# Twelve wide products of zeros in place of forty-eight narrow ones at the start of TensorE's stream

## The chip, the cores and the metric

The kernel runs on one core of a Trainium2 chip. The metric is the device time of one execution in microseconds (us), the median of several runs. Each core has TensorE (PE; its weight loads are listed apart as PEld), VectorE (DVE), ScalarE (ACT), GpSimd (POOL) and SyncE (SP, which issues nearly all the DMAs here). They run in parallel, each through its own list of instructions in order, and wait for one another by semaphores.

## The reference, cut to what matters

Two stages follow one another. The first is a linear attention with a decaying state, for 4 batches, 8 heads, 768 positions and a head of 48:

```python
for t in range(S):
    cur = np.einsum('bhd,bhe->bhde', u[None] * kt, vt)
    y[:, :, t] = np.einsum('bhd,bhde->bhe', rt, state + cur)
    state = wt[:, :, :, None] * state + np.einsum('bhd,bhe->bhde', kt, vt)
```

The second takes y as 3072 tokens of 384 numbers through two matrices (384 to 2048, 2048 to 384) with a piecewise quadratic gate between them:

```python
h = x @ w_in
g = np.where(h >= 1, h, np.where(h <= -1, 0.0, (h + 1) ** 2 / 4))
return g @ w_out
```

The products of zeros that this document is about are not part of either stage. They write zeros to PSUM banks before those are used.

## The kernel before, in words

Attention is done in 12 units of 256 positions (three for each batch), each in chunks of 64. For a unit, DVE scans the decays forward and backward (lines 439 and 434, tiles p and y) and scales r and k with the results (lines 518 and 468, tile rk). TensorE multiplies r and k within a chunk (line 488), transposes k (line 527), forms the states' updates (line 549) and then the outputs (line 598). The second stage takes 512 tokens at a time (256 in parts of the first blocks), and for each of 16 slices of the weights makes nine products into h (line 960) and nine into acc (line 980). Each number is split in two parts of lower precision, and three products of such parts are added. The weights are loaded raw and decoded once, on ACT, POOL and DVE (lines 356 to 369).

The order of instructions on each engine is set before the program runs, by a planner (class Plan). It is given a cost in us and a due time for each operation, goes through them as a machine with five engines would, and writes them out in the order in which they began there.

The change is in the first operation of TensorE, the function warm (lines 322 to 328), which the planner treats as one piece. It runs as soon as GpSimd has filled the tiles zero and clear with zeros. It makes SMALL products of the fp32 tile zero, each with 64 rows of weights and 64 columns of weights. Number n takes the upper or lower half of the partitions of zero by n % 2, and the upper or lower half of the output's partitions by n // 2 % 2. So four consecutive products use the four quarters of the array. All go to the first two banks. Then one product of 128x128 by 512 columns goes to each of the 8 PSUM banks (the function cleared, line 331). Wherever the planner sees a gap on TensorE of over 0.5 us, it puts further products of line 331 in (functions kept_warm and zeros).

The planner's cost of warm is a constant, 0.16 + 0.054 * SMALL + 0.43 * 8. The profile has two of line 331's products ahead of the ones of line 325, and six more behind the eight of warm.

Of the kernel before, what the change touches and what calls it, by code (L numbers as in the profile page):

```python
# [24 lines left out]
C = 64  # L25
NC = UT // C
SEG = 2 * (UT + 1)
HP = 64
# [9 lines left out]

LAG = 2
IDLE, FILLED, ZEROS = 0.5, 0.72, 0.235  # L40
SMALL = 48

LANES = 8

# [195 lines left out]
def attention_moe(tc, a):  # L240
    nc = tc.nc
    V, A, G, PE = nc.vector, nc.scalar, nc.gpsimd, nc.tensor
# [7 lines left out]
    def tiles(n, shape, dt, name, of=pool):  # L250
        return [of.tile(shape, dt, tag=f"{name}{i}", name=f"{name}{i}") for i in range(n)]

    def one(shape, dt, name, of=pool):
        return tiles(1, shape, dt, name, of)[0]
# [10 lines left out]
    zero = one([128, 128], F32, "zero")  # L265
    clear = one([128, 128], F32R, "clear")
# [25 lines left out]
    bank = [*tiles(3, [128, 512], F32, "bank", psum), *acc, *hp]  # L292

    def op(engine, cost, due, reads, writes, emit, **kw):
        return plan.add(engine, cost, emit, due, reads, writes, **kw)
# [8 lines left out]
    SOON = 0, 200.0  # L304
# [17 lines left out]
    def warm():  # L322
        for n in range(SMALL):
            g, h = n // 2 % 2, n % 2
            PE.matmul(bank[h][HP * g : HP * g + C, 0:C], lhsT=zero[HP * h : HP * h + HP, 0:C], rhs=zero[HP * h : HP * h + HP, 0:C],
                      start=True, stop=True)
        for b in bank:
            cleared(b, 4)

    def cleared(out, n):  # L330
        PE.matmul(out[:, 0 : 128 * n], lhsT=clear, rhs=clear.unsqueeze(1).broadcast_to([128, n, 128]), start=True, stop=True)  # L331

    op("PE", 0.16 + 0.054 * SMALL + 0.43 * 8, SOON, ["zero", "clear"], [("b", i) for i in range(8)], warm)

    def zeros(b, us):
        halves = int(FILLED * us / ZEROS * 2)
# [713 lines left out]
```

## Time and profile before

| | us |
|---|---|
| median of 3 runs | 505.94 |
| lowest and highest run | 504.72, 509.08 |
| profiled execution, its own time | 508.8 |
| span of that execution, first to last instruction | 507.1 |
| TensorE busy in the span | 492.8 |
| VectorE busy | 332.2 |
| ScalarE busy | 296.1 |
| GpSimd busy | 100.4 |

The profile is of one execution. Its span begins with its first instruction, and every position given in this document counts from there. The time of an execution is 1.7 us longer than its span, for what lies around the first and the last instruction. An fp32 product stands in the profile as two matmul records and two weight loads, so that the 48 products of line 325 are 96 records.

### The profile page before, as it was taken

What the parts mean: (1) busy time and instruction counts of PE and PEld (TensorE: products, weight loads), DVE (VectorE), ACT (ScalarE), POOL (GpSimd) and SP (SyncE); (2) the same over time, 40 slices, a digit from 0 to 9 for tenths busy, and PEclk for the clock granted to TensorE, in tenths of its full rate; (3) what the DMA queues carried; (4) which work ended last, traced back from release to release, by engine and by line L of the source; (5) the groups of instructions that cost most, each with busy time, mean ns of one, the idle gap of its engine ahead of it and who ended that gap; (6) DMA issues with size and microseconds to landing.
All of it is one profiled execution on the core that took longest, in us unless ns stands there. A gap on an engine that the chain in (4) does not pass through costs nothing.

```text
span 507.1 us, 13246 instructions
## 1 busy us (share of the span) xinstructions
PE 492.8 (97%) x5562; PEld 412.5 (81%) x5562; DVE 332.2 (66%) x560; ACT 296.1 (58%) x605; POOL 100.4 (20%) x68
## 2 busy tenths in 40 slices
PE   8999999999999999999999899999999999999995
PEld 6778987889999988888878678888887888888884
DVE  6899997956998699849555979842364333243331
ACT  3597798987875564745643565653454444454441
POOL 2487766801012321102001112100010000000000
PEclk9999999999999999999999999999999999999999
DMA  8984734326643434505006342300110000100001
GB/s 297 403 296 147 281 145 153 126 64 208 201 126 97 140 108 143 167 11 204 23 1 193 106 134 90 123 1 1 63 49 13 17 1 0 63 2 0 1 1 67
DMA packets 21922, 54.12 MB, mean 107 GB/s; under 512 B 3104, under 2 KB 8672, under 8 KB 21856
## 3 DMA queue, kind: packets, MB, share of 16 engines
q1 hardware_dynamic: 21856, 53.21, 31.5%
q8 instruction: 45, 0.74, 0.6%
q14 instruction: 21, 0.17, 0.1%
HBM read 46.32 MB, written 4.72 MB: 101 GB/s over the span
## 4 chain that ended last, share of the span: by engine, by line
PE 75%; DVE 13%; DMA 4%; ACT 3%; issue 3%; SPq 1%; ACTq 0%; DVEq 0%
PE h L960 33%; PE acc L980 33%; PE bank L598 4%; DVE y L434 2%; DVE gl L768 2%; PE bank L488 2%; DMA rk<-in_rk 2%; DVE p L439 1%; DMA wraw<-in_wbits 1%; DVE wt L369 1%; PE bank L527 1%; PE bank L549 1%; DVE r L494 1%; DMA wq<-in_w 1%; DVE g L765 1%
## 5 line engine op out<-in xcount | busy, mean ns | idle before, releaser
L960 PE MATMUL h<-x,wt 128*128 128x512 f32 (+1 forms) x1008 | 216.8, 361 | 1.9 <-DVE g L765 1.3
L960 PEld LDWEIGHTS h<-x,wt 128*128 128x128 f32 x1008 | 168.3, 188 | 31.8 <-DVE g L765 1.9
L980 PE MATMUL acc<-gh,wt 128*128 128x512 f32 (+1 forms) x672 | 152.2, 360 | 0.0
L980 PEld LDWEIGHTS acc<-gh,wt 128*128 128x128 f32 x672 | 113.8, 188 | 19.0
L765 DVE SCALAR_TENSOR_TENSOR g<-g,h 128x512 f32<-128x512 f32 (+1 forms) x112 | 67.4, 605 | 92.1 <-ACT g L764 84.9
L763 ACT ACTIVATE g<-h 128x512 f32<-128x512 f32 (+1 forms) x112 | 59.7, 533 | 85.8 <-PE h L960 84.1
L768 DVE TENSOR_TENSOR gl<-g,gh 128x512 fp32r<-128x512 f32 (+1 forms) x112 | 73.3, 659 | 28.9 <-ACT gh L767 13.5
L767 ACT CAST gh<-g 128x512 fp32r<-128x512 f32 (+1 forms) x112 | 62.1, 558 | 39.6 <-PE acc L980 18.6
L980 PE MATMUL acc<-gl,wt 128*128 128x512 f32 (+1 forms) x336 | 84.5, 357 | 0.1
L980 PEld LDWEIGHTS acc<-gl,wt 128*128 128x128 f32 x336 | 58.4, 187 | 10.0 <-DVE gl L768 0.5
L764 ACT ACTIVATE g<-g 128x512 f32<-128x512 f32 (+1 forms) x112 | 64.0, 571 | 3.3
L364 POOL TENSOR_SCALAR rr<-wraw 128x768 uint16<-128x768 f32 x16 | 52.7, 3291 | 35.0 <-DVE fl L366 17.3
L514 POOL TENSOR_TENSOR r<-cst,d 128x512 f32<-128x512 f32 x16 | 17.3, 1104 | 157.0 <-PE bank L598 131.9
L506 POOL TENSOR_TENSOR nk<-nk 128x768 f32<-128x768 f32 x8 | 16.8, 2096 | 83.7 <-DMA nk<-in_nk 74.5
L439 DVE TENSOR_TENSOR_SCAN p<-wq,seeds 128x514 f32<-128x514 f32 x24 | 30.2, 1259 | 3.7 <-DMA wq<-in_w 2.8
L434 DVE TENSOR_TENSOR_SCAN y<-wq,seeds 128x514 f32<-128x514 f32 x24 | 30.8, 1282 | 0.8
L468 DVE TENSOR_TENSOR rk<-rk,y 128x512 f32<-128x512 f32 x24 | 18.9, 789 | 3.1 <-DMA rk<-in_rk 2.9
L331 PE MATMUL bank<-clear 128*128 128x512 f32 (+1 forms) x57 | 17.1, 418 | 1.8 <-DVE seeds L438 1.8
L369 DVE TENSOR_TENSOR wt<-fl,wt 128x768 fp32r<-128x768 f32 x16 | 16.5, 1033 | 3.2 <-ACT wt L356 3.1
L598 PEld LDWEIGHTS bank<-rk,st 48*48 48x48 f32 (+1 forms) x656 | 11.4, 121 | 8.6 <-DVE st L567 2.9
L363 ACT ACTIVATE rr<-wraw 128x768 uint16<-128x768 uint32 x16 | 17.5, 1094 | 1.1 <-DVE fl L366 1.1
L518 DVE TENSOR_TENSOR rk<-rk,p 128x512 f32<-128x512 f32 x24 | 17.7, 749 | 0.2 <-PE acc L488 0.2
(108 smaller groups left out, 384.5 us busy)
## 6 DMA issues: line engine op xcount, KB each, us to landing
rk<-in_rk SPq DMA_DIRECT2D x24, 512.0 KB, 4.8
wraw<-in_wbits SPq DMA_DIRECT2D x16, 768.0 KB, 7.9
wq<-in_w SPq DMA_DIRECT2D x24, 257.5 KB, 3.3
nk<-in_nk SPq DMA_DIRECT2D x8, 768.0 KB, 4.8
vn<-in_v SPq DMA_DIRECT2D x11, 384.0 KB, 5.8
fl<-in_w SPq DMA_DIRECT2D x12, 257.0 KB, 2.9
out_y<-g SPq DMA_DIRECT2D x11, 256.0 KB, 2.3
x<-last SPq DMA_DIRECT2D x66, 32.0 KB, 2.5
```

The source lines that it names most:

```text
L364: op("POOL", 3.35, due, [("raw", f)], ["rr_high"], lambda: G.tensor_scalar(out=r16[:, :, 1], in0=wraw[f][:, :, 1].bitcast(F32), scalar1=0. ...
L369: op("DVE", 0.95, due, [("fl", k), ("wh", f)], [("wl", f)], lambda: V.tensor_tensor(out=w_lo[f], in0=s, in1=w_hi[f].bitcast(F32), op=ALU.s ...
L434: V.tensor_tensor_scan(out=y_[:, ::-1], data0=w[:, SEG:0:-1], data1=sv[:, ::-1], initial=0.0, op0=ALU.mult, op1=ALU.add)
L439: V.tensor_tensor_scan(out=pv[:, q].rearrange("p n c -> p (n c)"), data0=w[:, 0:SEG], data1=sv, initial=0.0, op0=ALU.mult, op1=ALU.add,)
L598: PE.matmul(out=bank[by[g]][HP * half : HP * half + wide, lo : lo + C], start=first, stop=False, skip_group_check=True, **kw)
L763: op("ACT", c, due, [("b", 6 + hk)], [("g", gk)], lambda: nc.scalar.activation(gs, hs, AF.Relu, scale=0.5, bias=0.5))
L764: op("ACT", c, due, (), [("g", gk)], lambda: nc.scalar.activation(gs, gs, AF.Square))
L765: op("DVE", 0.13 + 0.56 * k, due, [("b", 6 + hk)], [("g", gk)], lambda: nc.vector.scalar_tensor_tensor(out=gs, in0=gs, scalar=1.0, in1=hs, ...
L767: op("ACT", c, due, [("g", gk)], [("gh", gk)], lambda: nc.scalar.copy(ghs, gs))
L768: op("DVE", 0.18 + 0.52 * k, due, [("g", gk), ("gh", gk)], [("gl", gk)], lambda: nc.vector.tensor_tensor(out=gls, in0=gs, in1=ghs.bitcast( ...
L960: nc.tensor.matmul(by16(hp, f), lhsT=wx[f][:, cs], rhs=by16(xt[:, j, :], f), start=n == 0, stop=n == 8)
L980: nc.tensor.matmul(by16(o[j]), lhsT=wx[f][:, cs], rhs=by16(gt), start=first and i == 0, stop=stop and i == 2, skip_group_check=True)
```

## The change

The number of the first products goes from 48 to 12, and each streams 256 columns in place of 64. The 256 columns are the same 64 columns of the tile zero, read four times over by a broadcast dimension. The weights, the halves of the partitions and the two banks that are written stay as they are; in these banks the columns 0 to 255 are written now, and not only 0 to 63. The planner's cost for each is four times what it was, so that the sum of warm comes out as before: 0.054 * 48 and 0.216 * 12 are both 2.592.

```diff
-SMALL = 48
+SMALL = 12
...
         for n in range(SMALL):
             g, h = n // 2 % 2, n % 2
-            PE.matmul(bank[h][HP * g : HP * g + C, 0:C], lhsT=zero[HP * h : HP * h + HP, 0:C], rhs=zero[HP * h : HP * h + HP, 0:C],
-                      start=True, stop=True)
+            PE.matmul(bank[h][HP * g : HP * g + C, 0 : 4 * C], lhsT=zero[HP * h : HP * h + HP, 0:C],
+                      rhs=zero[HP * h : HP * h + HP, 0:C].unsqueeze(1).broadcast_to([HP, 4, C]), start=True, stop=True)
...
-    op("PE", 0.16 + 0.054 * SMALL + 0.43 * 8, SOON, ["zero", "clear"], [("b", i) for i in range(8)], warm)
+    op("PE", 0.16 + 0.216 * SMALL + 0.43 * 8, SOON, ["zero", "clear"], [("b", i) for i in range(8)], warm)
```

TensorE's list becomes 36 products shorter at this one place. Everything before and behind it on TensorE, and the lists of the other four engines, stand in the same order as before; only the running numbers of some buffers differ.

## Rows read from the trace of the kernel before

**Rows 1.** The page, busy time of each engine, share of the span, instructions.
```profile
PE 492.8 (97%) x5562; PEld 412.5 (81%) x5562; DVE 332.2 (66%) x560; ACT 296.1 (58%) x605; POOL 100.4 (20%) x68
```
**Rows 2.** The chain of waits that ended last, stretch 0 to 20, pieces (start, us, what).
```profile
5.47 6.68 DMA wq<-in_w
...
12.25 1.24 DVE p L439
...
13.71 1.23 DVE y L434
14.94 0.27 DVE rk L518
```
**Rows 3.** Busy time by stretch: from:to us, length, engines' busy us (instructions), PEclk, DMA.
```profile
0.00:50.00 50.00, 45.37 (x902) 37.93 (x902) 42.73 (x71) 32.46 (x69) 28.32 (x29) 1.00 0.80 289
...
400.00:450.00 50.00, 50.00 (x223) 41.00 (x222) 16.74 (x26) 22.39 (x38) 0.00 (x0) 1.00 0.06 20
```
**Rows 4.** Timeline, PE, stretch 0 to 22: start, us, operation, count [idle before <-releaser].
```profile
1.79 1.22 PE L331 MATMUL bank<-clear 128*128 128x512 f32 x2 [1.79 <-DVE seeds L438]
...
2.94 2.84 PE L325 MATMUL bank<-zero 64*64 64x64 f32 x96
...
5.71 1.44 PE L331 MATMUL bank<-clear 128*128 128x512 f32 x3
...
8.13 1.53 PE L331 MATMUL bank<-clear 128*128 128x512 f32 x6
...
9.49 0.60 PE L527 MATMUL bank<-cst,rk 128*128 128x128 f32 x4
...
10.02 1.16 PE L488 MATMUL acc<-rk,nk 64*64 64x64 f32 x64
```
**Rows 5.** Line 325 by itself: duration ns min/median/max, first and last start.
```profile
L325 PEld LDWEIGHTS bank<-zero x96: 178/223/228, 2.9 to 5.4; 64*64 64x64 f32 x96
L325 PE MATMUL bank<-zero x96: 310/311/366, 2.9 to 5.5; 64*64 64x64 f32 x96
```
**Rows 6.** Timeline, PE, stretch 2.9 to 3.0: the first records of line 325.
```profile
2.94 0.39 PE L325 MATMUL bank<-zero 64*64 64x64 f32 x4
```
**Rows 7.** Timeline, PE, stretch 5.7 to 6.0: the last records of line 325.
```profile
5.45 0.33 PE L325 MATMUL bank<-zero 64*64 64x64 f32 x4
```
**Rows 8.** Timeline, PE, narrow stretches from 6.6 to 7.25: starts of line 331's products.
```profile
6.31 0.85 PE L331 MATMUL bank<-clear 128*128 128x512 f32 x2
...
6.73 0.42 PE L331 MATMUL bank<-clear 128*128 128x512 f32 x1
...
6.99 0.62 PE L331 MATMUL acc<-clear 128*128 128x512 f32 x2
...
7.22 0.61 PE L331 MATMUL acc<-clear 128*128 128x512 f32 x2
```
**Rows 9.** Timeline, PE, stretch 460 to 475: a slice of the second stage.
```profile
460.78 2.21 PE L960 MATMUL h<-x,wt 128*128 128x512 f32 x9
462.82 1.51 PE L980 MATMUL acc<-gh,wt 128*128 128x512 f32 x6
```
**Rows 10.** Timeline, DVE, stretch 8 to 17.
```profile
8.28 0.69 DVE L468 TENSOR_TENSOR rk<-rk,y 128x512 f32<-128x512 f32 x1
...
11.25 0.69 DVE L518 TENSOR_TENSOR rk<-rk,p 128x512 f32<-128x512 f32 x1 [0.15 <-PE acc L488]
11.89 0.06 DVE L438 MEMSET seeds<- 128x2 f32 x1
12.25 1.23 DVE L439 TENSOR_TENSOR_SCAN p<-wq,seeds 128x514 f32<-128x514 f32 x1 [0.30 <-DMA wq<-in_w]
...
16.73 0.33 DVE L565 COPY ob<-h 128x192 f32<-128x192 f32 x1
```
**Rows 11.** Timeline, ACT, stretch 7 to 12.6.
```profile
8.55 0.91 ACT L459 ACTIVATE nk<-rk,cst 128x256 f32<-128x256 f32 x2
...
11.85 0.59 ACT L534 COPY kt<-bank 128x512 f32<-128x512 f32 x1 [1.13 <-PE bank L527]
```
**Rows 12.** Timeline, PE, stretch 0 to 22: the filling products ahead of 15.6 and what follows.
```profile
13.35 1.66 PE L331 MATMUL bank<-clear 128*128 128x512 f32 x6
...
15.58 0.27 PE L488 MATMUL acc<-rk 64*64 64x64 f32 x1 [0.57 <-DVE seeds L438]
```

## The prediction, made before the changed kernel was run

> **What bounds the kernel now.** I read the busy times first. TensorE is busy for 97% of the span and no other engine for over 66% [rows 1], so over the whole kernel it is TensorE's work that sets the time. But the change touches only the first 6 us, and an average over 507 us says nothing of those. The table by stretches shows the difference: from 400 to 450 TensorE is busy without a gap while DVE has 16.74 us of work in 50; in the first 50 us DVE has 42.73 and the DMA engines are 80% busy [rows 3]. So I read the chain of waits for the start. There it doesn't pass through TensorE: it runs along the queue of loads to a load of wq, issued at 5.47 and landed 6.68 us later at 12.15, and from 12.25 along DVE's scans [rows 2]. What the first products of zeros do matters to the end only if they make TensorE so late that DVE waits for it.
>
> The third view is the timeline of TensorE. Two products of line 331 start at 1.79, then the 96 records of line 325 run from 2.94, line 331 is back at 5.71, 14 of its products run up to 9.49, and there the first real work begins, transposes of line 527 and then line 488 at 10.02 [rows 4]. The reader should see that there is no idle time noted between 2.94 and 9.49: TensorE goes from one thing to the next, so what the first products lose or gain shifts line 527 and line 488 by the same amount.
>
> The fourth view is DVE's timeline, for how much of a shift it bears. DVE's line 518 waits 0.15 us for the products of line 488 at 11.25, its next scan (line 439) starts at 12.25 and had waited 0.30 us for the load of wq [rows 10]. So TensorE may be 0.30 us later than now at no cost; every us beyond that makes the scan at 12.25 late, and that scan is on the chain [rows 2].
>
> **The change, part by part.**
>
> *Columns streamed.* 48 products of 64 columns are 3,072 columns, 12 of 256 are 3,072 too. What has to be found is whether TensorE takes them at the same rate. Four records start within the first 0.1 us [rows 6] and the last four start together at 5.45 [rows 7], so the 96 records are 24 groups of four, 23 steps in 5.45 - 2.94 = 2.51 us, 0.109 us for a group. Each record takes 0.311 us by itself [rows 5]: in a group four run side by side, one on each quarter of the array, and the next group follows before they end. A group streams 64 columns; 0.109 us is 1.7 ns a column.
>
> *The same with 256 columns.* The 12 products make 24 records, if each again stands as two, so 6 groups of four. At the rate above a group of 256 columns takes 4 x 0.109 = 0.436 us and six take 2.62, as 24 x 0.109 = 2.62 did. The trace of before has no product of a quarter of the array with over 64 columns, so this rate has to be bounded. From below: nothing in the rows makes a column cheaper in a longer product. If the 24 groups hold a fixed part, it goes down with 6; a step as the clock alone gives it is 64 columns at two cycles each, 0.107 us at 1.2 GHz (the two cycles are my reading of the rows, an estimate: 0.109 us for 64 columns at the level that line 331 shows, below), so at most 24 x 0.002 = 0.05 us is to be gained. From above: the four quarters no longer work side by side, and each record's 256 columns go by themselves, 24 x 0.436 = 10.5 us. I take 2.6 us, since groups of four are what the same quarters, weights and banks show, and keep both ends. That the columns are one block of 64 read four times costs nothing: line 331 reads a block of 128 four times over and its products follow one another every 0.23 us [rows 8], as those of line 960, which read 512 different columns, do (9 in 462.82 - 460.78 = 2.04 us, 0.227 each) [rows 9].
>
> *Weight loads.* 72 of the 96 loads go. Each took 0.223 us [rows 5] but 96 fit into 2.5 us, so they ran side by side and under the products; a group's four loads have 0.436 us to hide under now, in place of 0.109. Nothing is saved, nothing exposed.
>
> *The start and the turn behind it.* From the last group's start at 5.45 to line 331 at 5.71 are 0.26 us, of which 0.11 are the group's own columns and 0.15 the turn to the whole array. That stays. So the last of six groups starts at about 2.94 + 5 x 0.436 = 5.12 and line 331 at 5.12 + 0.436 + 0.15 = 5.71, the time of now, give or take 0.1.
>
> *The clock.* The granted clock reads 1.00 in every stretch [rows 3], but the starts of line 331 show both levels: 6.31 to 6.73 is 0.42 us for 512 columns, the lower level of 1.2 GHz; 6.73 to 6.99 is 0.26, and 6.99 to 7.22 is 0.23, the upper level of 2.4 GHz [rows 8]. It rose between 6.73 and 6.99, and ahead of that TensorE had been busy without a break since 1.79 but for the turn at 2.94. The new products keep it as busy, over the same time, so I take the same rise. The column of the page doesn't show the lower level here; the spacing decides.
>
> *The other engines.* Their lists stand in the same order, the planner's cost of warm is the same number, and nobody waits for line 325 but TensorE's own next products. The columns 64 to 255 that are now written too lie in banks that line 331 overwrites right after.
>
> **The sum.** 0.0 us on TensorE (from -0.05 to +0.1), all of it under the 0.30 us that DVE bears: 0.0 at the end. Against the profiled execution, 508.8 us with a span of 507.1, that is 508.8. That execution lies 2.9 us above the median of 505.94, near the highest run; the change moves neither, so the forecast for the median is **505.9 us**.
>
> **A rule that speaks against the change.** The rows show four loads and four products of four quarters at once [rows 5, 6]. The Trainium skill, "TensorE: Matmul & The Clock Gate", section "The mechanism", states that a weight load overlaps with products in flight only if its group of rows differs; here products n and n + 2 have the same rows. By that rule only two would run at once; the trace speaks against it at 64 columns, since 48 pairs of 0.109 us would be 5.2 us and not 2.5, and no run here shows 256. "TensorEngine Tiling (Array Packing)", section "Key Properties", has the four quarters of 64x64 load and multiply in parallel, which is what the rows show.
>
> **The rivals.**
>
> 1. *Two at a time.* With longer products, a product must let the one two places ahead finish. For: the profile has no such product of 256 columns. Against: the four at once at 64. Then 12 pairs of 0.436 us: nine by 6.87, when the clock has risen, three more at half of that, 0.65, to 7.5, and line 331 from 7.65. Its 14 products at 0.227 us end at 10.8 in place of 9.49, 1.3 us late, 1.0 beyond what DVE bears: 506.9. If the loads of 0.22 us were bare besides, 12 x 0.22 = 2.6 more: 509.6.
>
> 2. *One at a time, the case on the slower side.* The quarters don't overlap at all. Nine records by 6.87, then 15 at 0.218 = 3.3 to 10.1, line 331 from 10.3, its end at 13.5, 4.0 us late, 3.7 beyond the 0.30: 509.6. If a quarter of the array at work is also too little to raise the clock, 24 x 0.436 = 10.5 to 13.4, 14 products at 0.42 to 19.4: 9.9 late, 515.5. It is slower by over 1% only if TensorE comes over 5.4 us late, so if both happen.
>
> 3. *The clock rises at another time.* If it counts something of which there is four times less now (products, loads), it rises later. At the worst it stays low until the zeros are over: 14 x 0.42 = 5.9 from 5.85, 11.7 in place of 9.49, 2.2 us late: 507.8. If it rises earlier, all 14 could take 0.227 and end at 8.9; but line 527 needs DVE's line 468, which ends at 8.97 [rows 10], line 488 needs ACT's line 459, which ends at 9.46 [rows 11], and DVE's scan waits for wq to 12.15 in any case [rows 2]. So no gain: 505.9.
>
> What comes later bears more: the second transposes are copied by ACT at 11.85 [rows 11], their products feed DVE's line 565 at 16.73 [rows 10], and TensorE has filling products from 13.35 and 0.57 us idle before 15.58 [rows 12]. A way to over 1% faster I don't find: all of line 325 is 2.8 us, 0.55%, and it isn't on the chain.
>
> **How the numbers follow.** 1% is 5 us, about what a measurement of this kernel can tell from no change. The forecast gets 0.84, rival 1 0.05, rival 2 0.03, rival 3 0.06, and 0.02 are for what I don't see. The three runs shown span 504.72 to 509.08 by themselves, and that, not the change, makes the range: 503.5, a little under the lowest, since another median of a few runs may come out there, to 509.5, which takes in rivals 1 and 3 and the milder half of 2. Within 1%: the forecast, rivals 1 and 3, the milder half of 2, less what the scatter of runs may add, 0.92. Slower by over 1%: the harsher half of rival 2 and what is unseen or scatter, 0.05. Faster by over 1%: scatter alone, 0.03.
>
> **What would show it.** Line 325 has 24 records in 6 groups, 0.43 us apart, and line 331 is back at 5.6 to 5.8: the rate is right. If it is back at 7.5 or 10, rival 1 or 2. If its products are still 0.42 us apart behind 7.3, rival 3. If line 488 starts at 10.0 and DVE's scan of 12.25 still waits for wq, the cover was there. A scan that waits for TensorE, or a time beyond 511, makes the prediction wrong.

## The result, and the profile after

The changed kernel is slower by a little: 1.0064 of the time before, 95% interval 1.0041 to 1.0088. The medians are 510.24 us against 507.35, 14 runs of each. That is within 1%, as forecast, but outside the predicted range (its upper end was 509.5), and it is a real loss of 2.9 us (1.0041 to 1.0088 of 507.35 is 2.1 to 4.5 us) where none was forecast.

The profiled execution took 510.54 us with a span of 508.9, 1.8 us more than the span of before. First TensorE's timeline of the changed kernel, to be read beside [rows 4]:

```profile
2.95 2.84 PE L325 MATMUL bank<-zero 64*64 64x256 f32 x24
...
5.72 1.65 PE L331 MATMUL bank<-clear 128*128 128x512 f32 x3
...
8.69 1.52 PE L331 MATMUL bank<-clear 128*128 128x512 f32 x6
...
10.05 0.60 PE L527 MATMUL bank<-cst,rk 128*128 128x128 f32 x4
...
10.58 1.16 PE L488 MATMUL acc<-rk,nk 64*64 64x64 f32 x64
```

The 24 records take the 2.8 us that the 96 took, and line 331 is back at 5.72. But its first three products take 1.65 us and not 1.44: the clock rose later. The record of the granted clock has the upper level from 8.0 us on, and from 6.8 in the kernel before. So TensorE is 0.55 us late at line 527. VectorE's timeline, beside [rows 10], shows what that cost:

```profile
11.81 0.69 DVE L518 TENSOR_TENSOR rk<-rk,p 128x512 f32<-128x512 f32 x1 [0.69 <-PE acc L488]
12.45 0.06 DVE L438 MEMSET seeds<- 128x2 f32 x1
12.54 1.23 DVE L439 TENSOR_TENSOR_SCAN p<-wq,seeds 128x514 f32<-128x514 f32 x1
```

The scan starts at 12.54 and not 12.25, and has no wait for the load any more: it is 0.29 us late, near the 0.25 that 0.55 less the 0.30 of cover would leave. A clock that rises late is a loss of 0.3 us here, and not of 3.

The larger loss stands in the waits of TensorE. This view (line, releaser, us in total, times, longest) has two entries that the view of the kernel before doesn't have:

```profile
PE acc L598 <- issue: 1.3, 1, 1.3
...
PE acc L488 <- issue: 0.3, 1, 0.3
```

"Issue" is a wait for nothing that the profile shows. The first stands in TensorE's timeline, in the middle of a row of products of the same kind:

```profile
21.40 0.76 PE L598 MATMUL acc<-r,g 64*64 64x64 f32 x38
23.43 0.57 PE L598 MATMUL acc<-r,g 64*64 64x64 f32 x22 [1.26 <-issue]
```

38 products follow one another without a gap, then TensorE does nothing for 1.26 us, and the 22 others follow. The chain of waits that ended last passes through this wait (start, us, what):

```profile
20.96 1.21 PE acc L598 x63
22.16 1.26 issue
23.43 0.63 PE acc L598 x22
```

ScalarE (ACT) waits for exactly these products. Its timeline before, from 22.59:

```profile
22.59 0.42 ACT L678 COPY g<-acc 128x128 f32<-128x128 f32 x2
...
25.00 0.92 ACT L459 ACTIVATE nk<-rk,cst 128x256 f32<-128x256 f32 x2
```

and after:

```profile
24.04 0.44 ACT L678 COPY g<-acc 128x128 f32<-128x128 f32 x2 [1.06 <-PE acc L598]
...
26.46 0.93 ACT L459 ACTIVATE nk<-rk,cst 128x256 f32<-128x256 f32 x2
```

ACT is 1.45 us late from there on, and DVE's line 468, which needs ACT's line 459, starts at 27.42 and not at 25.95.

What runs dry is TensorE's list of instructions. Two DMA queues of the page carry nothing but instructions, q14 with 21 packets and 0.17 MB, and this one, the same before and after:

```profile
q8 instruction: 45, 0.74, 0.6%
```

45 packets of 16 KB. If an instruction takes 64 bytes (an estimate: 45 packets hold 11,520 of that size, and the trace before has 11,124 loads and products), a packet holds 256. That q8 is TensorE's goes by this count; two kernels below with 112 and 64 records more have 46 packets there. Now count TensorE's records up to the two waits. The table by stretches gives products and loads in brackets, first PE, then PEld; here for the changed kernel from the start up to just ahead of each wait's end:

```profile
0.00:16.90 16.90, 14.44 (x222) 10.03 (x222) 12.06 (x19) 4.97 (x11) 3.21 (x21) 1.00 0.91 332
0.00:23.40 23.40, 19.64 (x350) 14.17 (x350) 17.52 (x30) 8.75 (x18) 7.50 (x22) 1.00 0.94 348
```

222 + 222 = 444 and 350 + 350 = 700: the waits are 256 records apart. TensorE stops where a block of instructions ends; that the next has not come is what the packets below show. The Trainium skill, "Runtime: NRT & Kernel Launch", section "Instruction fetch mechanics", has an engine refill its instructions in 16 KiB blocks of 256 and fetch the next while it executes the present one; the count agrees. The Trainium skill, in the same section, calls the cost of a block's end mostly hidden; here 1.26 us of it are bare, so the measurement decides.

The queue's packet can be placed too. Of the stretches 16.95 to 20.8, 20.8 to 22.0 and 22.0 to 26 of the changed kernel, the DMA view has an instruction packet in the second alone:

```profile
q8 instruction: 1, 0.02, 5.7%
```

TensorE enters the block at 16.95, the packet of the one behind it begins at 20.84, 3.9 us later, and TensorE goes on at 23.42 (the load ahead of the product in the row), 2.6 us after the packet began and 6.47 after it entered. Until then it has to have work for the 256 records of the block. The same holds wherever it stood still: at all 16 such waits in the eight traces that have them, here and below, TensorE goes on 2.3 to 2.6 us after a packet on q8 began. In traces without a wait the packet was earlier: TensorE came to the end of a block 3.1 us after it in the kernel before (19.52), 2.8 in its second trace (19.19). Meanwhile all DMA engines are busy with data, a share of 1.02 in the column before the last (a transfer counts whole where it begins, so that it can pass 1); at a later block's end, at 43.49, the share is 0.04:

```profile
16.90:20.80 3.90, 3.84 (x62) 3.00 (x62) 3.80 (x9) 2.95 (x6) 3.09 (x1) 1.00 1.02 390
...
43.40:44.20 0.80, 0.80 (x72) 0.80 (x61) 0.77 (x3) 0.79 (x1) 0.00 (x0) 1.00 0.04 10
```

There the packet begins at 44.24, 0.75 us after TensorE entered the block.

### The profile page after: what moved, and what is told of

Read it like the earlier page. It is cut to its first block, busy times and chain, and to the rows that moved or that the text cites. A ratio compares the mean times of both kernels' runs of the same rounds, so it can differ in the third digit from the quotient of the medians.

```text
span 508.9 us, 13102 instructions
## 1 busy us (share of the span) xinstructions
PE 493.1 (97%) x5490; PEld 411.8 (81%) x5490; DVE 331.4 (65%) x560; ACT 296.1 (58%) x605; POOL 100.3 (20%) x68
## 4 chain that ended last, share of the span: by engine, by line
PE 77%; DVE 11%; ACT 5%; issue 3%; DMA 2%; SPq 0%; ACTq 0%; POOL 0%; DVEq 0%; POOLq 0%
PE acc L980 33%; PE h L960 33%; PE bank L598 4%; DMA rk<-in_rk 2%; PE bank L488 2%; DVE wt L369 1%; DVE y L434 1%; DVE p L439 1%; PE bank L331 1%; DVE r L494 1%; PE bank L527 1%; DVE g L765 1%; PE bank L549 1%; DVE gl L768 1%; ACT rr L363 1%
## 5 line engine op out<-in xcount | busy, mean ns | idle before, releaser
L768 DVE TENSOR_TENSOR gl<-g,gh 128x512 fp32r<-128x512 f32 (+1 forms) x112 | 71.6, 644 | 29.2 <-ACT gh L767 13.8
```

What stands on the lines that cost most here:

```text
L768: op("DVE", 0.18 + 0.52 * k, due, [("g", gk), ("gh", gk)], [("gl", gk)], lambda: nc.vector.tensor_tensor(out=gls, in0=gs, in1=ghs.bitcast( ...
```

## The experiments

Each kernel ran beside the kernel before on the same chip. All keep the planner's cost for the first products at 2.592 us, so that nothing else moves.

**76 narrow products.** 304 records, 112 more than before, so that blocks end where they do in the changed kernel.

```diff
-        for n in range(SMALL):
+        for n in range(76):
...
-            PE.matmul(bank[h][HP * g : HP * g + C, 0:C], lhsT=..., rhs=zero[HP * h : HP * h + HP, 0:C],
+            PE.matmul(bank[h][HP * g : HP * g + C, 0:40], lhsT=..., rhs=zero[HP * h : HP * h + HP, 0:40],
```

> 76 products of 40 columns (3,040 columns, 304 records) in place of 48 of 64. Two theories. Instruction blocks: TensorE's instructions come in blocks of 256 (16 KB), one per record; with 112 records more than before the blocks end at the same places of the program as with 12 of 256 (144 fewer; 112 + 144 = 256), so TensorE should again stand still without a releaser in line 598 near 22 us for about 1.3 us, and the time should be that of the changed kernel, about 1.006 of before (510 us). Clock: if the changed kernel is slower because long and few products raise TensorE's clock later, many short ones raise it no later than before, no stall in line 598, and the time is 0.998 to 1.001 of before (507 us).

Measured: 1.0056 (1.0035 to 1.0077). The waits are back in the same two places of the program:

```profile
18.76 0.27 PE L488 MATMUL acc<-rk 64*64 64x64 f32 x1 [0.59 <-issue]
...
25.23 0.57 PE L598 MATMUL acc<-r,g 64*64 64x64 f32 x22 [1.13 <-issue]
```

The second is again ahead of the last 22 products of line 598. But the test is not clean: I took the group of four to get shorter with its columns, and it doesn't.

```profile
2.95 4.29 PE L325 MATMUL bank<-zero 64*64 64x40 f32 x152
7.17 1.65 PE L331 MATMUL bank<-clear 128*128 128x512 f32 x3
```

38 groups take 0.107 us each, as with 64 columns, and TensorE is 2.05 us late at line 527 (11.54). Lateness and dry spots can't be told apart in its time.

**8 long and 40 very short products.** 192 records as before.

```diff
-        for n in range(SMALL):
+        for n in range(8):
...
+            PE.matmul(bank[h][HP * g : HP * g + C, 0 : 4 * C], lhsT=..., rhs=...unsqueeze(1).broadcast_to([HP, 4, C]),
...
+        for n in range(40):
...
+            PE.matmul(bank[h][HP * g : HP * g + C, 0:8], lhsT=..., rhs=zero[HP * h : HP * h + HP, 0:8],
```

> 8 products of 256 columns and 40 of 8 columns: 48 products and 192 records as before, but two thirds of the columns in long products as in the changed kernel. Instruction blocks: blocks end where they did before, no stall in line 598, time within 0.2% of before. Clock: the long products raise the clock as late as in the changed kernel and the time is 1.003 to 1.007 of before.

Measured: 1.0045 (1.0024 to 1.0065), and no wait of a product on "issue". Again the short products took as long as longer ones (40 of them 2.2 us), line 331 came back at 6.90, the clock rose at 10.75, and TensorE reached the transposes at 11.98, 2.49 us late. So both theories are half right here: the dry spots are gone with the old count of records, and TensorE's lateness costs about what the prediction's cover gives, 2.49 - 0.30 = 2.2 us (DVE's scan starts at 14.48, 2.23 late); measured 510.50 against 507.79, 2.7. So a late start of another kind costs much the same.

**12 products of 64 columns.** As few records as the changed kernel, but TensorE is early.

```diff
-        for n in range(SMALL):
+        for n in range(12):
```

> 12 products of 64 columns: as few instructions as the changed kernel, but a quarter of the columns, so line 331 comes about 1.9 us earlier than before and TensorE is early at 9.5 us. Instruction blocks: they end where they do in the changed kernel; the stall in line 488 near 17 us may go since TensorE reached the block before earlier, the one in line 598 near 22 us stays, 0.8 to 1.5 us; time 1.002 to 1.006 of before although TensorE starts earlier. Clock: TensorE cannot be late at 9.5 us whatever the clock does, so time 0.998 to 1.000 of before.

Measured: 1.0044 (1.0024 to 1.0065). This one tells them apart. TensorE waits for DVE ahead of line 527, 0.57 us earlier than in the kernel before, so no clock can have made it late, and the waits stand where they do in the changed kernel:

```profile
8.92 0.66 PE L527 MATMUL bank<-cst,rk 128*128 128x128 f32 x4 [0.17 <-DVE rk L468]
...
16.18 0.27 PE L488 MATMUL acc<-rk 64*64 64x64 f32 x1 [0.41 <-issue]
...
22.65 0.57 PE L598 MATMUL acc<-r,g 64*64 64x64 f32 x22 [1.26 <-issue]
```

**64 products of 48 columns.** 64 records more than before.

```diff
-        for n in range(SMALL):
+        for n in range(64):
...
-            PE.matmul(bank[h][HP * g : HP * g + C, 0:C], lhsT=..., rhs=zero[HP * h : HP * h + HP, 0:C],
+            PE.matmul(bank[h][HP * g : HP * g + C, 0:48], lhsT=..., rhs=zero[HP * h : HP * h + HP, 0:48],
```

> 64 products of 48 columns (3,072 columns, 256 records, 64 more than before). Instruction blocks: from the times at which TensorE of before reached each record, blocks would now be entered at 12.5, 16.5 and 22.4 us; about 6.3 us are needed from entering one block to having the one after the next (as the changed kernel shows, 16.95 to 23.42), so TensorE runs dry in line 488 near 16.5 us for some 2 us and a little again near 22; time 1.003 to 1.008 of before. Clock: more and shorter products than before, so 0.998 to 1.001.

Measured: 1.0057 (1.0036 to 1.0079). TensorE starts line 527 at 9.53, as before (9.49), and the waits have moved in the program, as forecast from the block ends, though the first is shorter than the 2 us expected:

```profile
17.29 0.27 PE L488 MATMUL acc<-rk 64*64 64x64 f32 x1 [0.79 <-issue]
...
23.76 0.73 PE L331 MATMUL bank<-clear 128*128 128x512 f32 x2 [0.60 <-issue]
```

Counted in records they have not moved by one (350 + 350 and 478 + 478, again 700 and the next one 256 on):

```profile
0.00:17.25 17.25, 14.27 (x350) 11.55 (x350) 12.85 (x22) 5.58 (x13) 3.45 (x21) 1.00 0.91 327
0.00:23.70 23.70, 20.13 (x478) 16.00 (x478) 18.09 (x30) 10.03 (x21) 8.13 (x22) 1.00 0.94 346
```

**The changed kernel with its records put back.** The 12 long products stay; 39 narrow ones (156 records) take the place of the six filling products (12 records) ahead of line 527.

```diff
         for b in bank:
             cleared(b, 4)
+        for n in range(39):
+            g, h = n // 2 % 2, n % 2
+            PE.matmul(bank[h][HP * g : HP * g + C, 0:C], lhsT=..., rhs=zero[HP * h : HP * h + HP, 0:C],
...
     def zeros(b, us):
+        calls.append(b)
+        if len(calls) == 2:
+            return
```

> The changed kernel's 12 products of 256 columns, and 39 narrow ones (64 columns) behind line 331's eight, in the place of the six filling products ahead of line 527. So the long products stay, but from line 527 on the blocks of instructions end where they do before the change (48 + 156 records here, 192 + 12 there). Instruction blocks: no stall without a releaser in lines 488 and 598, time 1.000 to 1.002 of before. Wide products by themselves (by the clock or by anything else in them): as the changed kernel, 1.004 to 1.009.

Measured: 1.0015 (0.9998 to 1.0033), 508.51 us. Three quarters of the loss are gone (0.0015 left of 0.0064) with the same long products, but not as expected: two waits remain, at the block ends of the kernel before (this kernel's line numbers are nine higher: its 558, 607 and 687 are 549, 598 and 678 here):

```profile
14.96 0.24 PE L558 MATMUL h<-g,kt 64*48 64x48 f32 x1 [1.71 <-issue]
...
21.16 0.33 PE L607 MATMUL acc<-rk,ob 48*64 48x64 f32 x3 [0.47 <-issue]
```

I had expected none. The narrow products come later than in the kernel before, so TensorE enters its blocks later (9.15 and not 5.36) and passes faster through the first (5.81 us and not 7.53). Nor are these waits harmless in this trace. ACT is 1.28 us late (22.59 before), much as in the changed kernel:

```profile
23.87 0.43 ACT L687 COPY g<-acc 128x128 f32<-128x128 f32 x2 [1.29 <-PE acc L607]
```

DVE is 1.12 us late at 42 us, where the changed kernel has 1.28. So the run shows that long products don't cost 1.0064 by themselves, but not that the time came back because the waits went; the profiled execution is the longest of its twelve (509.66 us), and whether the others ran dry too isn't known. That stays open.

**The kernel before once more**, unchanged.

> The kernel before, unchanged, for a second trace and for the scatter: 0.999 to 1.001, no stall in lines 488 and 598; the clock may rise at another time than 6.8 us, and if TensorE is late by that, DVE's line 518 waits longer than 0.15 us.

Measured: 0.9997 (0.9980 to 1.0013). The clock rose at 6.0 us, line 527 started at 9.13, DVE's line 518 didn't wait, and no product waits on "issue".

**The kernel before without the six filling products**, with 48 and with 51 narrow ones.

```diff
     def zeros(b, us):
+        calls.append(b)
+        if len(calls) == 2:
+            return
...
-        for n in range(SMALL):
+        for n in range(51):
```

The last two lines are the second kernel's alone.

> The kernel before without the six filling products of line 331 ahead of line 527 (12 records fewer, so that blocks end 12 records later in the program). TensorE then reaches line 527 1.3 us earlier and waits there for DVE's line 468 (8.97 us), so a clock that rises late costs nothing. Blocks are entered at about 12.9, 20 and 28 us, no stall. If the kernel before loses time to a late clock in part of its executions: 0.997 to 0.999, and less scatter. If lateness of that size doesn't matter: 1.000.

> As the run without the six filling products, with 51 in place of 48 narrow ones, which puts the 12 records back, so blocks end exactly where they do before the change: 0.997 to 0.999 if lateness at 9.5 us matters in the kernel before, 1.000 if not. If this one is as before and the run with 48 is not, the 12 records made the difference.

Measured, with 48 and with 51: 0.9999 (0.9985 to 1.0012) and 0.9999 (0.9984 to 1.0015). In their traces TensorE waits 2.44 and 1.76 us for DVE ahead of line 527, and no product waits on "issue". So TensorE's lateness at line 527 costs the kernel before nothing that these runs can show, and the scatter stays (506.06 to 508.69 and 506.08 to 509.50 us). Neither beats it.

**The changed kernel without the six filling products.**

```diff
     def zeros(b, us):
+        calls.append(b)
+        if len(calls) == 2:
+            return
```

> The changed kernel (12 products of 256 columns) without the six filling products ahead of line 527. TensorE has 1.3 us to spare there, so a clock that rises late costs little or nothing, but the blocks of instructions end only 12 records later than in the changed kernel, the third still inside or right behind line 598's products near 22 us. Instruction blocks: TensorE runs dry there again for about a us, time 1.003 to 1.006 of before. Clock: 0.999 to 1.001. What lies between this run and the changed kernel's 1.0064 is the part of a late clock.

Measured: 1.0045 (1.0029 to 1.0061). TensorE waits 1.52 us for DVE ahead of line 527, so the clock's rise (8.1 us) is covered, and the waits are there, 12 records on in the program: 16 and not 22 products of line 598 (line 603 in this kernel) are left behind the stop.

```profile
17.71 0.27 PE L493 MATMUL h<-rk 64*64 64x64 f32 x1 [0.30 <-issue]
...
23.91 0.46 PE L603 MATMUL acc<-r,g 64*64 64x64 f32 x16 [0.98 <-issue]
```

This is the cleanest pair: with 48 narrow products (the run above) and with 12 long ones, both without the six filling products and with TensorE waiting for DVE at line 527, the time is 0.9999 and 1.0045; the kernel with 12 products of 64 columns (1.0044) shows that their length isn't needed for it. Between 1.0045 and the changed kernel's 1.0064 may be a part of a late clock; the intervals overlap, and that stays open.

**The changed kernel twice more**, unchanged.

> The changed kernel, unchanged, for a second trace: the clock may rise at another time than 7.96 us, while the stalls in line 488 near 17 us and in line 598 near 22 us should be there again, the second 1.1 to 1.5 us. If the stalls are an accident of one execution they are gone or elsewhere.

> The changed kernel, unchanged, for a third trace: as the second one. If long products raise the clock later by their kind, all three rise later than 6.8 us; if the moment is chance, one of them rises as early as in the kernel before (6.0 and 6.8 us in its two traces).

Measured: 510.69 and 508.83 us, one execution each. The first, where the clock rose at 6.2 us and line 527 started at 9.23:

```profile
16.27 0.27 PE L488 MATMUL acc<-rk 64*64 64x64 f32 x1 [0.42 <-issue]
22.74 0.57 PE L598 MATMUL acc<-r,g 64*64 64x64 f32 x22 [1.25 <-issue]
```

The second, where it rose at 5.0, within the long products, and line 331 was back at 5.40:

```profile
16.24 0.27 PE L488 MATMUL acc<-rk 64*64 64x64 f32 x1 [0.44 <-issue]
22.44 0.57 PE L598 MATMUL acc<-r,g 64*64 64x64 f32 x22 [0.99 <-issue]
```

The waits are in every trace; the clock's rise moves: 8.0, 6.2 and 5.0 us in three executions of the changed kernel, 6.8 and 6.0 in two of the kernel before. So it isn't always later with long products; five executions say no more.

## Why the prediction was wrong

*What held.* The columns: 24 records in 2.84 us, line 331 at 5.72 for a predicted 5.71. The four quarters work side by side with 256 columns, so rivals 1 and 2 didn't come true. The weight loads hide. The turn stays. The cover on DVE is about 0.3 us, as 0.55 us of lateness became 0.29. The order of all lists is the same.

*The clock.* I took the same rise at 6.8 us. In the profiled execution it was 8.0, rival 3 in part, and that is 0.3 us of this execution's loss by DVE's scan. But the moment is chance in both kernels, and an execution in which it came early was slow just the same (510.69 us with a rise at 6.2). (Rival 3 counts the turn twice in its start at 5.85; from 5.71 its worst case is 507.7 and not 507.8, which changes nothing.)

*The starting point.* From the forecast of 505.9 to 510.24 are 4.3 us, and 1.4 of them are the kernel before's: its median is 507.35 over 14 runs, and 505.94 over the three that the forecast was built on. The change made the other 2.9. Nor is 1% "about what a measurement of this kernel can tell from no change": the interval here is 0.5% wide.

*The step that failed* is the one in the first paragraph on which the sum stands: "What the first products of zeros do matters to the end only if they make TensorE so late that DVE waits for it." With it goes the term on weight loads, "72 of the 96 loads go [...] Nothing is saved, nothing exposed", and so the 0.0 at the end. I counted what the removed records did on the array and under the products, and left out that each is an instruction that has to be fetched; that term stood at nothing without a reason. With 144 records fewer, every later block of 256 ends 144 records later in the program. Before, TensorE entered blocks at 12.89, 19.52 and 28.29 us (the starts of the records that stand at the block ends), 6.63 and 8.78 us apart, and each had come in time. After, it entered them at 11.32, 16.95 and 23.42: the stretches in between are made of rows of 64x64 products (lines 488 and 598), of which TensorE takes 256 records in some 2 us where it has the operands (an estimate: 38 products and their loads in 0.76 us), and it stands still for 0.28 and 1.26 us. With 12 products of 64 columns TensorE was early, and the same two waits came with 1.0044. The page has the queue with its 45 packets, 0.6% of the DMA engines' time; it should have been read as a supply on which every instruction of TensorE depends.

*The rivals* all had TensorE late by its own first products. None had it wait later. The price behind "over 1% only if TensorE comes over 5.4 us late" was tried only up to 2.49 us, where 8 long and 40 very short products cost 2.7 us; the time did stay within 1%.

*From 1.3 us to 3.* DVE's instructions, compared one by one between the two profiled executions, stand 1.28 us later at 42 us. At 186 us a second loss shows. GpSimd's line 506, before:

```profile
185.82 2.71 POOL L506 TENSOR_TENSOR nk<-nk 128x768 f32<-128x768 f32 x1 [10.74 <-DMA nk<-in_nk]
```

and after, where it started 1.3 us earlier, with DVE's line 468 in the same stretch:

```profile
184.51 2.50 POOL L506 TENSOR_TENSOR nk<-nk 128x768 f32<-128x768 f32 x1 [9.01 <-DMA nk<-in_nk]
```

```profile
L468 DVE TENSOR_TENSOR rk<-rk,y x1: 2249/2249/2249, 185.3 to 185.3; 128x512 f32<-128x512 f32 x1
```

Line 468 takes 2.25 us where it took 0.67 before, when GpSimd began after it. DVE is 0.42 us late ahead of it and 2.0 behind it; by 220 us 1.4 are left, and at the end of the list 2.1. In the third trace of the changed kernel only 0.3 are left there. Such meetings are no mark of the changed kernel alone: the kernel before has one at 236.75 us, where its line 468 takes 2.27. But near 186 us all nine traces of kernels that came out above 1.001 have one, on line 468 or on the scan of line 434 (2.66 and 2.70 in place of 1.23), and the four traces at 1.000 have none. The nine include the kernel with 8 long and 40 very short products, which never ran dry and was late for another reason. So a late start by either cause goes together with this second loss, and how one brings the other is open.

What is shown, then: another count of records costs time though TensorE isn't late at line 527, and TensorE runs dry at block ends. The waits' direct price is some 1.0 us in the profiled execution (DVE is 0.27 us late at 20 us and 1.28 at 42), about a third of the 2.9. How the rest adds up is read from traces only, and I didn't try it by itself. Nor did I try to make the fetch faster by emptier DMA queues: that the wait is long because the engines are full is read from the two stretches above.

## What to carry to other kernels

Instructions are a supply like data: where an engine issues hundreds of small products in a few us while the DMA engines are full, look at where its blocks of 256 end, and at waits on "issue" in the middle of a row of equal instructions. A change in the number of instructions anywhere ahead moves all later block ends, so take such a change for one that acts far from its place, and compare at the same count modulo 256 before the edit itself is blamed or praised; the kernel with its records put back shows that the count alone is not enough, since it also matters when TensorE comes to a block. When the operation's own time comes out as predicted and the kernel's doesn't, count records up to the new waits.

## What the runs showed of the hardware that was not expected

- From the start of the instruction packet to TensorE's going on 2.3 to 2.6 us, at 16 waits in eight traces (DMA share 0.84 to 1.05 in the blocks ahead of them). From the end of one such wait to the end of the next, one block later, 6.47 us in five traces (16.95 to 23.42, 16.27 to 22.74, 16.18 to 22.65, 18.76 to 25.23, 17.29 to 23.76) and 6.20 in three (16.24 to 22.44, 17.71 to 23.91, 14.96 to 21.16). From a block entered without a wait to the end of the first wait it was 4.8 to 5.9 us, so 6.47 is no fixed time of a fetch; in the second trace of the kernel before two entries 6.34 us apart went without one.
- A group of four 64x64 fp32 records takes 0.107 us at the lower clock level with 64, 48, 40 or 8 columns: fewer columns than 64 save nothing there. With 256 it takes 0.427, four times as long.
- A DVE product of 128x512 took 2.25 us in place of 0.67 where GpSimd's product of 128x768 had begun 0.8 us ahead of it, and 2.27 in the kernel before at 236.75, where that was 0.1 us.
